# Seven block products instead of eight in the whole experts of a state-space and router kernel

## The chip, the cores and the metric

The kernel runs on one core of a Trainium2 chip. The metric is the device time of one execution in microseconds (us). Three runs of the kernel before took 296.1, 296.74 and 298.02 us; the median is 296.74. A further execution was profiled; all rows below are from it.

In the profile PE is TensorE (PEld its weight loads), DVE is VectorE, ACT is ScalarE, POOL is GpSimd, SP is SyncE, which issues most loads.

## The reference: what is computed

A Mamba-2 state-space block (4 batches, 8 heads, 768 steps) produces 3072 tokens of 256 values. A cosine router sends each token to one of 8 experts, and the expert is a multilayer perceptron (MLP) of two layers, 256 to 1024 to 256:

```python
logits = xn @ en.T / tau
expert_idx = np.argmax(logits, axis=1)
...
gate_w = probs[np.arange(N), expert_idx]
for e in range(E):
    mask = expert_idx == e
    h = np.maximum(x[mask] @ w1[e], 0.0)
    out[mask] = gate_w[mask, None] * (h @ w2[e])
```

All of it is in 32-bit floating point.

## The kernel before, in words

The first 97 us compute the state-space block and the routing, and scatter the tokens into a table in DRAM, sorted by expert. This stage isn't changed. The change lies in the stage behind it, `moe` (L789).

Each expert has 416 places: 4 tiles of 104 tokens. The work is cut into ten parts. Parts 0 to 3 are half experts (experts 0 and 1, two tiles or 208 tokens each; the first half starts before all tokens are routed). Parts 4 to 9 are the six whole experts 2 to 7, 416 tokens each. Tokens that don't fit would go through `leftover` (L899), a loop whose number of turns is read from a table that `leftover_blocks` (L841) computes on VectorE. With this data the loop makes no turn, but its branch is executed.

A part (`part`, L803) runs in an order written out by hand; inside `manual_schedule` every engine executes its instructions in the order of the code:

- **First layer**, `up` (L734): for each of 8 blocks of 128 hidden values, two matmuls (the 256 inputs are two halves of 128) into a PSUM tile `hp`. ReLU moves the result to SBUF as `hT`, on ScalarE (L744) for even blocks and on VectorE (L746) for odd ones.
- Between the blocks, `out` (L768) turns the results of the part before back to rows, scales them by the gate on VectorE (L776) and ScalarE (L778), and writes them to DRAM with an indirect DMA issued by GpSimd (L780).
- `measure` (L682 on) prepares the gate: squares on ScalarE (L692) and a `pow` on GpSimd (L696).
- `turn_x` (L716) transposes the tokens of the next part on TensorE and copies them to SBUF on VectorE (L727).
- `prepare` (L700 on) finishes the gate: some ten small VectorE instructions, with an Exp on ScalarE (L710) among them.
- **Second layer**, `down` (L748): for each half of the 256 outputs, 8 matmuls into a PSUM tile `yp`, copied to SBUF by ScalarE (L762) and VectorE (L764).

Weights are loaded by SyncE three parts ahead (`load_weights`, L203). GpSimd does nothing in this stage but the `pow`, the indirect writes and a tiny memset before each write. In the last part the second layer is split by tokens, so that the rows of its first half are written while the second half is computed.

Of the kernel before, what the change touches and what calls it, by code (L numbers as in the profile page):

```python
# [8 lines left out]
F32 = mybir.dt.float32  # L9
I32 = mybir.dt.int32  # L10
BF16 = mybir.dt.bfloat16
ACT = mybir.ActivationFunctionType
ALU = mybir.AluOpType
# [10 lines left out]
KD, KF = DM // 128, F // 128  # L24
TR, NT = 104, 4
# [3 lines left out]
EE, EC, HT = 2, 4, 2  # L29
LEFT = (T - CAP) // Q + E  # L30

LG, Y1, TOK, W = 128, 128 + E, DM + E, DM + 2 * E
# [106 lines left out]
def between(k):  # L139


    nc = k.nc
    n = NC - 1
    ps = k.pz[:, 1, 448:512]
    for b in range(NB):
        nc.tensor.matmul(  # L146
            ps[:, 16 * b : 16 * b + 16], lhsT=k.spread[:, b, :], rhs=k.parts[:].rearrange("p v k g -> p (v k g)"),
            start=True, stop=True,
        )
    sides = k.mc.tile([128, NB, 2, 8], F32, name="sides")  # L150
    nc.vector.tensor_copy(out=sides[:].rearrange("p b v c -> p (b v c)"), in_=ps)
    k.whole = k.mc.tile([128, NB, n], F32, name="whole")
    nc.vector.tensor_tensor(out=k.whole[:], in0=sides[:, :, 0, 0:n], in1=sides[:, :, 1, 1:NC], op=ALU.mult)
    k.blocks = k.mc.tile([128, NB * n, 2 * 4], F32, name="blocks")
    nc.vector.tensor_tensor(
        out=k.blocks[:], in0=k.whole[:].rearrange("p b k -> p (b k)").unsqueeze(2).to_broadcast([128, NB * n, 8]),
        in1=k.own[:].rearrange("p v q -> p (v q)").unsqueeze(1).to_broadcast([128, NB * n, 8]), op=ALU.mult,
    )
# [44 lines left out]
def load_weights(k, e):  # L203
    k.w1t[e] = k.wp.tile([128, KD, F], F32, name="w1", tag="w1")
    k.nc.sync.dma_start(k.w1t[e][:], k.w1[e].rearrange("(k p) f -> p k f", p=128))
    k.w2t[e] = k.wp.tile([128, KF, DM], F32, name="w2", tag="w2")
    k.nc.sync.dma_start(k.w2t[e][:], k.w2[e].rearrange("(f p) m -> p f m", p=128))
# [449 lines left out]
class Job:  # L657
# [58 lines left out]
    def turn_x(s, ps=None):  # L716
        k, nc, tr, nt = s.k, s.k.nc, s.tr, s.nt
        s.xT = (s.pool or k.p).tile([128, KD, nt * tr], F32, name="xT", tag="xT")
        n = nt * tr
        for j in range(KD):  # L720
            t = s.turned()[:, 0:n] if ps is None else ps[:, n * j : n * j + n]
            for i in range(nt):
                nc.tensor.transpose(
                    t[:, tr * i : tr * i + tr], s.x[:, i, Y1 * j : Y1 * j + 128], k.ident[:tr, :tr]
                )
            if ps is None:
                nc.vector.tensor_copy(out=s.xT[:, j, :], in_=t)  # L727
        if ps is not None:
            nc.scalar.copy(out=s.xT[:].rearrange("p j n -> p (j n)"), in_=ps[:, 0 : KD * n])

    def turned(s):
        return s.k.ps.tile([128, 512], F32, name="turned", tag="turned", bufs=3)

    def up(s, f, ps=None):  # L734
        k, nc, n = s.k, s.k.nc, s.nt * s.tr
        if f == 0:
            s.hT = (s.pool or k.p).tile([128, KF, n], F32, name="hT", tag="hT")
        t = k.ps.tile([128, n], F32, name="hp", tag="hp", bufs=3)[:] if ps is None else ps[:, 0:n]
        for j in range(KD):
            nc.tensor.matmul(  # L740
                t, lhsT=s.w1[:, j, 128 * f : 128 * f + 128], rhs=s.xT[:, j, :], start=(j == 0), stop=(j == KD - 1)
            )
        if f % 2 == 0 or ps is not None:
            nc.scalar.activation(s.hT[:, f, :], t, ACT.Relu)  # L744
        else:
            nc.vector.tensor_scalar_max(s.hT[:, f, :], t, 0.0)  # L746

    def down(s, first, n, between=None):  # L748

        k, nc = s.k, s.k.nc  # L750
        if first == 0:
            s.yT = k.p.tile([128, KD, s.nt * s.tr], F32, name="yoT", tag="yoT")
        c = slice(s.tr * first, s.tr * (first + n))
        for j in range(KD):
            t = k.ps.tile([128, n * s.tr], F32, name="yp", tag="yp", bufs=2)
            for f in range(KF):
                nc.tensor.matmul(  # L757
                    t[:], lhsT=s.w2[:, f, 128 * j : 128 * j + 128], rhs=s.hT[:, f, c],
                    start=(f == 0), stop=(f == KF - 1),
                )  # L760
            if j % 2 == 0:
                nc.scalar.copy(out=s.yT[:, j, c], in_=t[:])  # L762
            else:
                nc.vector.tensor_copy(out=s.yT[:, j, c], in_=t[:])  # L764
            if j == 0 and between:
                between()

# [18 lines left out]
            k.tc.add_to_no_dep_group("out", d.ins)  # L786


def moe(k):  # L789
    parts = [(j, k.early_has[:TR, e, :]) for e, j in enumerate(k.early)]  # L790
    for e in range(EE):
        parts.append((Job(k, HT, TR, k.w1t[e], k.w2t[e]), k.late_has[:TR, e, :]))
    n = E + EE

    def begin(i):
        e = i - EE
        if e < EE:
            parts[i][0].load(k.p.tile([TR, HT, W], F32, name="xg", tag="xg"), T * e + HT * TR)
        else:
            parts.append((Job(k, NT, TR, k.w1t[e], k.w2t[e]), k.has[:TR, e - EE, :]))  # L800
            parts[i][0].load(k.p.tile([TR, NT, W], F32, name="xg", tag="xg"), T * e)

    def part(i):  # L803
        j, has = parts[i]
        last = parts[i - 1][0]
        for f in range(KF):
            j.up(f)
            if 1 <= f and 2 * (f - 1) < last.nt:
                last.out(2 * (f - 1), 2)
            if f == 3:  # L810
                j.measure()
        if i + 1 < n:
            parts[i + 1][0].turn_x()
        j.prepare(has)
        if i + 1 < n:
            j.down(0, j.nt)
        if i == EE + 2:
            leftover_blocks(k)
        if 0 <= i - EE < E - 3:
            load_weights(k, i - EE + 3)  # L820
        if i + 3 < n:
            begin(i + 3)

    with k.tc.manual_schedule():
        begin(EE)
        begin(EE + 1)
        parts[1][0].turn_x()
        parts[0][0].down(0, HT)
        for i in range(1, n - 2):
            part(i)  # L830
    leftover(k)
    with k.tc.manual_schedule():
        for i in range(n - 2, n):
            part(i)
        j = parts[n - 1][0]
        j.down(0, NT // 2)
        j.down(NT // 2, NT // 2, between=lambda: j.out(0, NT // 2))
        j.out(NT // 2, NT // 2)


def leftover_blocks(k):  # L841
# [57 lines left out]
def leftover(k):  # L899
    nc = k.nc  # L900
    table, rf, nf = k.left
    SP = mybir.EngineType.SP
    blocks = nc.values_load(table[0:1, 1, 0:1], min_val=0, max_val=LEFT)
    with k.tc.If(blocks > 0):  # L904
        with k.tc.For_i(0, blocks, 1) as i:
            e = nc.values_load(table[0:1, 0, bass.ds(i, 1)], engines=(SP,), min_val=0, max_val=E - 1)
            w1 = k.wp.tile([128, KD, F], F32, name="w1", tag="w1")
            nc.sync.dma_start(w1[:], k.w1[bass.ds(e, 1)].rearrange("o (k p) f -> p (o k) f", p=128))
            w2 = k.wp.tile([128, KF, DM], F32, name="w2", tag="w2")
            nc.sync.dma_start(w2[:], k.w2[bass.ds(e, 1)].rearrange("o (f p) m -> p (o f) m", p=128))  # L910
            j = Job(k, 1, Q, w1, w2)
            has = k.p.tile([128, 1], I32, name="left_has", tag="left_has")
            nc.vector.tensor_tensor(out=has[:], in0=k.part[:], in1=nf[:, bass.ds(i, 1)], op=ALU.is_lt)
            r = k.p.tile([128, 1], F32, name="left_p", tag="left_p")
            nc.vector.tensor_tensor(out=r[:], in0=k.part[:], in1=rf[:, bass.ds(i, 1)], op=ALU.add)
            at_f = k.p.tile([128, 1], F32, name="left_atf", tag="left_atf")
            nc.vector.memset(at_f[:], float(E * T))
            nc.vector.copy_predicated(at_f[:], has[:], r[:])
            at = k.p.tile([128, 1], I32, name="left_at", tag="left_at")
            nc.vector.tensor_copy(out=at[:], in_=at_f[:])  # L920
            x = k.p.tile([128, 1, W], F32, name="left_x", tag="left_x")
            nc.vector.memset(x[:], 1.0)
            j.gather(x, at)
            j.turn_x()
            j.measure()
            j.prepare(has[:])
            for f in range(KF):
                j.up(f)
            j.down(0, 1)
            j.out(0, 1)  # L930
# [88 lines left out]
```

## Time and profile before

| What | us |
|---|---|
| median of three runs | 296.74 |
| time of the profiled execution | 297.09 |
| its span, first to last instruction | 294.7 |
| state-space block and routing, up to the first second layer (97.44) | 97.4 |
| one whole expert, first layer with transposes (187.94 to 200.71) | 12.77 |
| one whole expert, second layer (200.71 to 211.90) | 11.19 |
| last matmul of a second layer ends | 285.35 |
| last indirect write issued until | 289.26 |

The span is what the profiler saw on the core; the time of the same execution is 2.4 us longer. The mean clock that TensorE was granted is 0.983 of full speed. A line such as `97.44 5.81 PE L757 MATMUL yp<-hT,w 128*128 128x208 f32 x32` gives start, duration from first start to last end, engine, source line, operation, output and inputs, tile, moving shape and number of records. A matmul in 32-bit floating point leaves two records, so x32 are 16 matmuls. Ends of matmuls are modelled and reach a little into the next one.

### The profile page before, as it was taken

Reading aid. Unit: us, or ns where it says so; the run is one execution under the profiler, and the core shown is the slowest. Engines: PE = TensorE matmul, PEld = TensorE weight load, DVE = VectorE, ACT = ScalarE, POOL = GpSimd, SP = SyncE. Lnnn points to the kernel's source line nnn. Section 1 sums busy time; section 2 is a strip of 40 time slices with the busy share of each in tenths; the row PEclk is TensorE's granted clock in tenths of the full one; section 3 lists DMA queues with packets and bytes.
Section 4 is the critical chain, followed back from the end, with each engine's and each line's share of the span. In section 5 each row is a group of like instructions: output and inputs, shape, how many; then the busy total and the mean of one; then the engine's idle time right before and its main releaser. Section 6 shows DMA issues by size and latency. Waiting matters only on the chain.

```text
span 294.7 us, 4832 instructions
## 1 busy us (share of the span) xinstructions
PE 266.5 (90%) x1828; PEld 192.8 (65%) x1828; DVE 125.8 (43%) x403; ACT 77.2 (26%) x211; POOL 93.0 (32%) x172
## 2 busy tenths in 40 slices
PE   0887999999887999999999999999999989999980
PEld 0665887887765899999555555555555545555970
DVE  7576897998622143423240743133034023212310
ACT  2312444533333131331410320040051023014110
POOL 8005436955345230330300070070051015007032
PEclk9999899999999999999999999999999999999995
DMA  6988398931131310385705416334352001001011
GB/s 170 364 308 295 106 362 287 398 130 53 64 101 57 118 31 0 80 281 176 234 11 196 142 47 208 90 113 104 108 174 57 20 3 49 0 0 56 2 29 29
DMA packets 18226, 37.24 MB, mean 126 GB/s; under 512 B 2042, under 2 KB 10439, under 8 KB 18202
## 3 DMA queue, kind: packets, MB, share of 16 engines
q1 hardware_dynamic: 15338, 30.36, 31.1%
q0 software_dynamic: 2688, 6.50, 6.8%
q8 instruction: 15, 0.25, 0.3%
q10 hardware_dynamic: 176, 0.06, 0.1%
q14 instruction: 9, 0.07, 0.1%
HBM read 26.80 MB, written 10.37 MB: 126 GB/s over the span
## 4 chain that ended last, share of the span: by engine, by line
issue 46%; PE 17%; POOL 14%; DMA 11%; DVE 9%; ACT 1%; POOLq 0%; ACTq 0%; DVEq 0%
DMA out_dram<-yo,to 11%; POOL out_dram L780 8%; PE pg L315 4%; DVE g L321 3%; PE pz L369 3%; PE py L351 3%; POOL rows L595 3%; POOL gr L696 2%; PE pf L250 2%; PE py L337 2%; DVE bp L224 1%; PE pf L268 1%; PE pz L234 1%; DMA a<-in_a_dram 1%; PE pz L146 1%
## 5 line engine op out<-in xcount | busy, mean ns | idle before, releaser
L757 PE MATMUL yp<-hT,w 128*128 128x208 f32 (+1 forms) x352 | 91.6, 418 | 0.0
L740 PE MATMUL hp<-xT,w 128*128 128x416 f32 (+1 forms) x288 | 88.0, 455 | 1.9 <-DVEq L904 1.4
L757 PEld LDWEIGHTS yp<-hT,w 128*128 128x128 f32 x352 | 63.5, 190 | 24.2 <-issue 24.2
L780 POOL DMA_INDIRECT out_dram<-yo,to x32 | 32.6, 1017 | 145.9 <-DVE yo L776 141.2
L740 PEld LDWEIGHTS hp<-xT,w 128*128 128x128 f32 x288 | 52.2, 190 | 29.3 <-issue 27.3
L746 DVE TENSOR_SCALAR hT<-hp 128x416 f32<-128x416 f32 (+1 forms) x36 | 18.7, 519 | 55.5 <-PE hp L740 50.3
L744 ACT ACTIVATE hT<-hp 128x416 f32<-128x416 f32 (+1 forms) x36 | 16.5, 459 | 76.6 <-PE hp L740 72.2
L764 DVE COPY yoT<-yp 128x208 f32<-128x208 f32 (+1 forms) x11 | 5.2, 473 | 63.1 <-PE yp L757 63.1
L595 POOL DMA_INDIRECT rows<-yt,row_of x24 | 23.8, 990 | 25.0 <-issue 12.1
L321 DVE TENSOR_TENSOR g<-pg,mask 128x1024 f32<-128x1024 f32 x24 | 28.2, 1218 | 5.6 <-PE pg L315 5.5
L315 PE MATMUL pg<-cm,bt 32*128 32x256 f32 x192 | 20.6, 450 | 0.0
L260 ACT ACTIVATE cm<-cp,tmask 128x256 f32<-128x256 f32 x24 | 10.9, 500 | 21.0 <-DVE cp L255 19.8
L369 PE MATMUL pz<-turn,yT 128*128 128x136 f32 x96 | 15.2, 304 | 1.0 <-ACT yT L361 1.0
L369 PEld LDWEIGHTS pz<-turn,yT 128*128 128x128 f32 x96 | 12.8, 201 | 4.9 <-issue 2.7
L315 PEld LDWEIGHTS pg<-cm,bt 32*128 32x128 f32 x192 | 14.4, 210 | 0.9 <-issue 0.7
L351 PE MATMUL py<-g,x 128*32 128x128 f32 x384 | 13.5, 277 | 0.2 <-issue 0.2
L762 ACT COPY yoT<-yp 128x208 f32<-128x208 f32 (+1 forms) x11 | 4.5, 411 | 30.6 <-PE yp L757 30.6
L297 POOL TENSOR_TENSOR T<-V,blocks 128x256 f32<-128x256 f32 x20 | 11.8, 618 | 0.0
L250 PE MATMUL pf<-f,spread 32*128 32x128 f32 x48 | 10.5, 349 | 1.2 <-DVE V L282 0.6
L692 ACT ACTIVATE sq<-xg 104x256 f32<-104x256 f32 x28 | 11.2, 406 | 0.0
L351 PEld LDWEIGHTS py<-g,x 128*32 128x32 f32 x384 | 10.4, 112 | 1.1 <-issue 0.5
L778 ACT ACTIVATE yo<-turned,gate 104x256 f32<-104x256 f32 x16 | 7.6, 473 | 13.6 <-PE turned L773 13.5
(174 smaller groups left out, 244.2 us busy)
## 6 DMA issues: line engine op xcount, KB each, us to landing
w<-in_moe_w_dram SPq DMA_DIRECT2D x16, 1024.0 KB
rows<-none SPq DMA_DIRECT2D x8, 442.0 KB
x<-in_x_dram SPq DMA_DIRECT2D x6, 512.0 KB
xg<-rows SPq DMA_DIRECT2D x6, 442.0 KB
b<-in_B_dram SPq DMA_DIRECT2D x6, 256.0 KB
ct<-in_CT_dram SPq DMA_DIRECT2D x6, 256.0 KB
out_dram<-yo,to POOLq DMA_INDIRECT x32
xe<-rows SPq DMA_DIRECT2D x2, 221.0 KB
```

The source lines that it names most:

```text
L250: nc.tensor.matmul(k.pf[:, 256 + 128 * i : 384 + 128 * i], lhsT=k.spread[g : g + 32, b + i, :], rhs=k.f[g : g + 32, c // 4, :], start=True ...
L297: k.nc.gpsimd.tensor_tensor(out=T[:], in0=k.V[c][:, b, :].rearrange("p (t d) -> p t d", t=2).unsqueeze(2).to_broadcast([128, 2, 4, D]), in ...
L315: nc.tensor.matmul(k.pg[:, q, 256 * i : 256 * i + 256], lhsT=s.bt[r, i, :], rhs=s.cm[r, i], start=True, stop=True, tile_position=(32 * q, 0),)
L321: nc.vector.tensor_tensor(out=g[:], in0=k.pg[:, :, 256 * i : 256 * i + 256].rearrange("p q (t i) -> p q t i", t=2), in1=k.mask[:].unsqueez ...
L351: k.nc.tensor.matmul(k.py[32 * q : 32 * q + 32, 2 * i + v, :], lhsT=t.x[:, b + i, n : n + 32], rhs=s.g[i][:, q, v, :], start=(c == 0 and i ...
L369: k.nc.tensor.matmul(k.pz[:, i, at : at + Y1], lhsT=yT[:, 2 * i + j, :], rhs=k.turn[:, j, :], start=(j == 0), stop=(j == 1), skip_group_ch ...
L595: d = nc.gpsimd.indirect_dma_start(out=k.rows[:, :], out_offset=bass.IndirectOffsetOnAxis(ap=k.to[g][:, u : u + 1], axis=0), in_=k.yt[:, N ...
L740: nc.tensor.matmul(t, lhsT=s.w1[:, j, 128 * f : 128 * f + 128], rhs=s.xT[:, j, :], start=(j == 0), stop=(j == KD - 1))
L744: nc.scalar.activation(s.hT[:, f, :], t, ACT.Relu)
L746: nc.vector.tensor_scalar_max(s.hT[:, f, :], t, 0.0)
L757: nc.tensor.matmul(t[:], lhsT=s.w2[:, f, 128 * j : 128 * j + 128], rhs=s.hT[:, f, c], start=(f == 0), stop=(f == KF - 1),)
L780: d = nc.gpsimd.indirect_dma_start(out=k.out[:, :], out_offset=bass.IndirectOffsetOnAxis(ap=s.to[:, i : i + 1], axis=0), in_=y[:], in_offs ...
```

## The change

The six whole experts (parts 4 to 9) get a job class of their own, `Seven`. Each of the two matrix products of the expert is seen as a product of 2 by 2 blocks, and is computed with seven block products and extra sums instead of eight block products (the Winograd form of Strassen's method):

- The **weights** are cut in four blocks a[0] to a[3]; four combinations m[0] to m[3] are computed on GpSimd (`mix`), for both layers, each instruction on 128 partitions x 512 values. The combinations for a part are ordered on GpSimd's queue at the start of the part before it.
- The **tokens** are cut in two by the input half and in two by token; four differences `dx` are computed on VectorE (`mix_x`) behind the copies of `turn_x`.
- `up` now works on four groups `g`. In each, seven matmuls of 208 columns go to four PSUM tiles; three of them add to a tile that has been read already (`first=False`). Five sums per group are done on VectorE, one copy and three ReLUs on ScalarE. One of the four result blocks gets its ReLU only where it is used.
- Between the layers, four differences `dh` of the hidden values are computed on VectorE (`mix_h`, 128 x 832 values each).
- `down` has seven products of four matmuls each, with two copies on ScalarE and five sums on VectorE. `measure` stands behind the second product, and the copies of the next part's tokens, its `mix_x` and `prepare` (all of `rest`) behind the fourth.

Around it: the PSUM tiles `hp` (3) and `yp` (2) become one ring `sum` of five; `hT` has one buffer; the copies of `turn_x` become a method `turn_copies`; `leftover_blocks` moves from the end of part 4 to the end of part 1; `leftover` is inside the manual schedule; the last part writes its four tiles of rows together at the end instead of two and two.

```diff
+class Seven(Job):
+    def mix(s, name, a):
+        m = s.k.p.tile([128, 4, KF // 2, 128], F32, name=name, tag=name)
+        for out, in0, in1, op in (
+            (m[:, 0], a[2], a[3], ALU.add), (m[:, 1], m[:, 0], a[0], ALU.subtract),
+            (m[:, 2], a[2], a[0], ALU.subtract), (m[:, 3], a[1], m[:, 1], ALU.subtract),
+        ):
+            s.k.nc.gpsimd.tensor_tensor(out=out, in0=in0, in1=in1, op=op)
+        return m
...
+    def mix_x(s):
...
+        for i, in0, in1 in ((0, b[1], b[0]), (1, b[1], b[3]), (2, b[3], d[:, 0]), (3, b[2], d[:, 2])):
+            nc.vector.tensor_tensor(out=d[:, i], in0=in0, in1=in1, op=ALU.subtract)
...
+    def add(s, in0, in1, out=None):
...
+        s.k.nc.vector.tensor_tensor(out=out, in0=in0, in1=in1, op=ALU.add)
+    def keep(s, ps):
...
+        s.k.nc.scalar.copy(out=out, in_=ps)
...
+    def up(s, g):
...
+        x, y, z, w = (s.sum()[:, 0:h] for _ in range(4))
+        s.product([g], x, a, 0, b, 0)
+        x1 = s.keep(x)
+        s.product([g], y, m, 1, d, 2)
+        q = s.add(y, x1)
+        s.product([g], z, m, 0, d, 0)
+        u = s.add(z, q)
+        s.product([g], w, m, 2, d, 1)
+        s.add(w, u, o[:, 3])
+        nc.scalar.activation(o[:, 3], o[:, 3], ACT.Relu)
+        s.product([g], x, a, 1, b, 2, False)
+        nc.scalar.activation(o[:, 0], x, ACT.Relu)
+        s.product([g], z, m, 3, b, 3, False)
+        s.add(z, q, o[:, 1])
+        s.product([g], w, a, 3, d, 3, False)
+        s.add(w, q, o[:, 2])
+        nc.scalar.activation(o[:, 2], o[:, 2], ACT.Relu)
+
+    def mix_h(s):
...
+        for i, j in ((0, 0), (1, 3)):
+            nc.vector.scalar_tensor_tensor(
+                out=d[:, i], in0=h[:, 1], scalar=0.0, in1=h[:, j], op0=ALU.max, op1=ALU.subtract
+            )
+        nc.vector.tensor_tensor(out=d[:, 2], in0=h[:, 3], in1=d[:, 0], op=ALU.subtract)
+        nc.vector.tensor_tensor(out=d[:, 3], in0=h[:, 2], in1=d[:, 2], op=ALU.subtract)
+
+    def down(s, measured, rest):
...
+        x, z, w, y = (s.sum()[:, 0:n] for _ in range(4))
+        s.product(gs, x, a, 0, b, 0)
+        x1 = s.keep(x)
+        s.product(gs, z, m, 0, d, 0)
+        z1 = s.keep(z)
+        measured()
+        s.product(gs, w, m, 2, d, 1)
+        t = s.add(w, z1)
+        s.product(gs, y, m, 1, d, 2)
+        q = s.add(y, x1)
+        s.add(t, q, o[3])
+        rest()
+        s.product(gs, x, a, 1, b, 2, False)
+        nc.scalar.copy(out=o[0], in_=x)
+        s.product(gs, w, a, 3, d, 3, False)
+        s.add(w, q, o[2])
+        s.product(gs, z, m, 3, b, 3, False)
+        s.add(z, q, o[1])
...
     def part(i):
...
+        if i == EE:
+            parts[2 * EE][0].mix_up()
+        elif new_seven:
+            if i >= 2 * EE:
+                new.mix_up()
+            new.mix_down()
...
-        if i == EE + 2:
+        if i == 1:
             leftover_blocks(k)
...
-        j = parts[n - 1][0]
-        j.down(0, NT // 2)
-        j.down(NT // 2, NT // 2, between=lambda: j.out(0, NT // 2))
-        j.out(NT // 2, NT // 2)
+        parts[n - 1][0].out(0, NT)
```

## The prediction

> **What bounds the kernel now.** I read the page's busy times first, then the table of stages, then TensorE's timeline. Columns of the stages: window, length, busy time (instructions) of PE, PEld, DVE, ACT, POOL, clock, DMA share, GB/s.
>
> ```profile
> PE 266.5 (90%) x1828; PEld 192.8 (65%) x1828; DVE 125.8 (43%) x403; ACT 77.2 (26%) x211; POOL 93.0 (32%) x172
> ...
> 187.94:200.71 12.77, 12.77 (x50) 7.51 (x48) 4.04 (x10) 4.53 (x14) 5.40 (x9) 1.00 0.38 115
> 200.71:211.90 11.19, 11.19 (x34) 6.10 (x33) 2.39 (x12) 0.74 (x2) 0.00 (x0) 1.00 0.43 134
> ...
> 97.44 5.81 PE L757 MATMUL yp<-hT,w 128*128 128x208 f32 x32
> 103.09 1.57 PE L740 MATMUL hp<-xT,w 128*128 128x208 f32 x8
> ...
> 151.99 11.36 PE L757 MATMUL yp<-hT,w 128*128 128x416 f32 x32
> 163.19 2.96 PE L740 MATMUL hp<-xT,w 128*128 128x416 f32 x8
> ```
>
> One whole expert takes 12.77 (first layer, transposes) + 11.19 (second) = 23.96 us. TensorE is busy through both at full clock; VectorE works 6.4 us of it, GpSimd 5.4. TensorE sets the pace, so a block product saved counts in full only if VectorE, ScalarE and GpSimd can follow.
>
> **Part 1, fewer multiplications.** 16 matmuls of 208 columns take 103.09-97.44 = 5.65 us, 0.353 each; 16 of 416 take 11.20, 0.700 each. (Each matmul leaves two records.) An expert goes from 32 x 0.700 = 22.40 to 56 x 0.353 = 19.77: 2.63 saved, 15.8 in six experts. TensorE alone would need 21.3 per expert.
>
> **Part 2, the circle inside a first layer.** Each group of seven products (7 x 0.353 = 2.47) now contains a chain. Prices: ScalarE copy or ReLU of 208, 0.33 (L762, 0.333) or 0.34; VectorE sum of 208, 0.38 (between 0.39 for 128x224, L850, and 0.37 for L746); the next dependent VectorE instruction 0.03 later (L850: 165.44, 0.38 long, next at 165.86); a wait across engines about 0.05 (ReLU ends 92.76, matmul starts 92.81); a result is read 0.20 after its matmul's slot (103.09 to 103.29). ScalarE takes its queue in order: the copy of the next group's x stands behind this group's last ReLU. So: keep x 0.33+0.05, q 0.38, u 0.41, o3 0.41+0.05, product w' 0.35+0.20, sum 0.38+0.05, ReLU 0.34, next keep: 2.95 us, against 2.47 of matmuls. In the two groups with output rows, a 0.47 scaling (L778) enters the circle: 3.4, against 2.47+0.43. Four groups: 2 x 3.4 + 2 x 2.95 = 12.7. With 0.7 of transposes and 28 x 0.353 = 9.9 an expert takes 23.3 if nothing waits at its end: only 0.7 of the 2.63 is left. The h differences, four of 128x832 at about 1.02 (by 0.39 for 224 and 1.21 for 1024 elements), hide under the transposes and the first products.
>
> **Part 3, VectorE's list in the second layer.** Times from that layer's start, D. The fourth product is read at D+5.85. Behind it in VectorE's order stand q and o3 (to 6.6), two copies (1.08 by L727: 7.7), four x differences (1.4: 9.1), preparation to the Exp (about 1.0: 10.1), Exp and its return (0.5), the gate (0.6: 11.2), and only then the last two sums, to 11.9. TensorE ends the layer at 9.9. The next layer's y needs the tile that ScalarE copies behind that Exp (10.9, due 10.3), z the tile of VectorE's last sum (11.9): some 1.4 lost, half of it slack of the circle's first group. 23.3 + 0.8 = 24.1: **an expert would cost what it does now**.
>
> **Part 4, GpSimd's sums stop VectorE.** Eight sums of 128x512 per expert come on GpSimd, where the next instruction behind the old `pow` is the next expert's first sum. The row that decides is in the first stage, where VectorE's L224 (two SBUF inputs, normally 0.275 to 0.284) met four GpSimd sums (L297):
>
> ```profile
> 54.10 2.38 POOL L297 TENSOR_TENSOR T<-V,blocks 128x256 f32<-128x256 f32 x4
> ...
> 54.03 1.97 DVE L224 TENSOR_TENSOR bp<-b,rT 128x128 f32<-128x128 f32 x1
> ...
> 54.03 2.59 DVE L224 TENSOR_TENSOR bp<-b,rT 128x128 f32<-128x128 f32 x2
> ...
> L321 DVE TENSOR_TENSOR g<-pg,mask x24: 1208/1215/1225, 16.9 to 77.8; 128x1024 f32<-128x1024 f32 x24
> ```
>
> Two that need about 0.5 together took 2.59. The first ran only near 55.8, after three of the four sums; the second ended at 56.62, after the fourth. The same shows at 64.77 (2.05 for the pair). L321, with one input in PSUM, keeps 1.21 to 1.23 throughout. So a VectorE instruction with two SBUF inputs waits for the sums already on their way. In the change these are o3, the x differences, the predicated copy and the small product of the preparation, and the h differences; sums from PSUM aren't.
>
> One GpSimd sum of 512: 0.61 for 256 elements (L297, every 0.57) bounds it by 1.22 above and, with 0.1 fixed as in a memset (0.09), by 1.04 below; I take 1.15, eight are 9.2. Every second one waits for the one before it, so they go as 1, 2, 2, 2, 1 with a gap where VectorE gets in. When: the second result is copied by D+3.4, four squares (144.91 to 146.5: 1.6) to 5.0, `pow` (1.05) to 6.1. The train begins just when o3 does. o3 waits to 7.25; copies to 8.7; x differences end at about 10.2, 12.8, 15.4 and 16.8; preparation, Exp and gate 2.1, last sums 0.75: 19.6 instead of 11.9. TensorE stands still for **7.5 us more**, at the start of whole experts 1 to 5, where each time the sums for the following one run (the sixth has none behind it). Before the first there is no o3, so some 6 there: 6 + 4 x 7.5 = 36. If GpSimd's instructions never queued and VectorE took turns with single ones, seven waits of at most 1.15 less what PSUM work covers, about 5.5 a time: 27. If the whole train went first, 9.2 + 6.1 + 3.2 + 2.9 = D+21.4: 9.5 a time, 47.
>
> [...]
>
> **Part 5, single items.** The list of leftover blocks (163.90 to 169.70: 5.8 on VectorE) moves from expert 2, where it cost TensorE 0.52 (170.34), into the last half expert, ahead of its second ReLU. That ReLU comes at 121.5 instead of 116.8; five sum tiles turn, the seventh product needs this tile at 119.8: 2.1, net +1.6 (0 to 3). The leftover branch: TensorE idles 1.38 now (237.40), and started 0.75 after VectorE's last copy; afterwards it starts as late behind VectorE's last sum: 0 to +1, I take 0.5. The weight loads and row loads that follow later preparation on SyncE have a whole expert's time ahead: 0. The merged PSUM pool frees no wait now visible: 0.
>
> The end: four rows now go out together.
>
> ```profile
> 286.17 0.48 DVE L776 TENSOR_SCALAR yo<-turned,gate 104x256 f32<-104x256 f32 x1 [0.41 <-PE turned L773]
> ...
> 286.95 1.00 POOL L780 DMA_INDIRECT out_dram<-yo,to  x1 [1.36 <-DVE yo L776]
> 287.94 0.09 POOL L779 MEMSET tick<- 1x1 f32 x1
> 288.26 1.00 POOL L780 DMA_INDIRECT out_dram<-yo,to  x1 [0.23 <-issue]
> ```
>
> Before, two follow the last product, 1.31 apart; four cost 2 x 1.31 = +2.6.
>
> **Sum.** 297.1 (profiled execution: span 294.7 and 2.4 around it; 0.35 over the median 296.74) + 6 x 0.15 (24.1 for 23.96) + 1.6 + 0.5 + 2.6 = 302.7 without part 4, and with its 36, 338.5. Against the median and for waits that overlap the branch I say **337**. Its own range: 27 to 47 in part 4 gives 329 to 349.
>
> **Rivals.** *The wait stays short:* the train and the x differences miss each other (GpSimd starts early or late) or GpSimd yields at once: 302, still slower, by the circle, the list and the tail. For it: the rows show the wait for 128x128 and 128x256 only. *Faster:* the multiplications alone bound it, because the circle runs faster than the rows add up to and no list waits: 297.1 - 15.8 + 1.6 + 0.5 + 2.6 = 286. It decides once a group's circle is under 2.47 and the train ends before D+6; against it stand 2.95 and `pow`'s place behind the squares. *Not what its title says:* GpSimd sums weights for the first layers only. The diff and the order of instructions show eight per expert, both layers; were it four, the wait would halve: 320. *The whole train goes first:* 349.
>
> **Chances.** The forecast (329 to 346) 0.66, the whole train or worse 0.09, half the wait 0.05, 302 (298 to 312) 0.14, faster 0.06. Range: 302 to 346. A measurement tells 1% from no change, 3 us: faster by over 1% 0.05, within 0.05, slower 0.90.
>
> **What would show it.** Right: x differences on VectorE, 0.38 alone, lasting 2 to 3 us beside GpSimd sums; TensorE idle 6 to 10 us after the first product of experts; groups 2.9 to 3.4 apart; GpSimd sums about 1.15; last four rows 1.31 apart. Wrong: x differences at 0.38 beside running sums, sums far from 1.15, groups 2.5 apart, or a train that starts long before D+6.

## The result, and the profile after

The changed kernel takes 337.51 us (median of four runs, 335.92 to 340.44) beside 296.42 for the kernel before on the same chip (295.47 to 298.02): a ratio of 1.139, 95% interval 1.128 to 1.150. It is slower, and 0.5 us from the forecast of 337. The experiments show that this closeness is partly luck: one term was too large, and one that the prediction doesn't have made up for it. Medians and ratios leave out the few runs that took over 1.5% more than the fastest of the same kernel.

The profiled execution took 340.44 us, with a span of 338.7, which is 44.0 more than before. The mean granted clock of TensorE is 0.929 (0.983 before). From the page, the busy times and the new sums on GpSimd:

```profile
PE 275.4 (81%) x2084; PEld 243.4 (72%) x2084; DVE 233.0 (69%) x570; ACT 95.6 (28%) x294; POOL 154.4 (46%) x220
...
L806 POOL TENSOR_TENSOR m<-w 128x512 f32<-128x512 f32 x24 | 31.6, 1317 | 1.4 <-DMA out_dram<-yo,to 1.4
```

TensorE's share falls from 90% to 81%. It waits more, and it is also busy for longer, though there is less to multiply. VectorE was busy for 125.8 us and now is for 233.0. A sum of this group takes 1.32 us as a mean.

Where did the 44.0 us go? The starts of the ten second layers, taken from the two TensorE timelines, tell it:

| from one second layer's start to the next | before | after | more |
|---|---|---|---|
| start of the program to the first (97.44, 98.37) | 97.44 | 98.37 | 0.93 |
| half experts 1, 2 and 3 together | 36.58 | 40.40 | 3.82 |
| into whole expert 1 | 17.97 | 24.15 | 6.18 |
| into whole expert 2 | 24.75 | 31.73 | 6.98 |
| into whole expert 3 | 23.97 | 31.44 | 7.47 |
| into whole expert 4 | 23.96 | 32.46 | 8.50 |
| into whole expert 5, with the leftover branch | 25.58 | 35.01 | 9.43 |
| into whole expert 6 | 23.24 | 23.24 | 0.00 |
| last second layer and end | 21.2 | 21.9 | 0.7 |

Five intervals hold 38.6 of it. Each holds the start of a first layer (whole experts 1 to 5) during which GpSimd computes the combinations for the following expert. Into expert 6 no combinations are computed, and nothing is lost. TensorE's timeline of one such start (start, duration, operation, in brackets the idle time before it and what ended it; the second layer begins at D = 194.65):

```profile
203.12 1.57 PE L829 MATMUL sum<-h,m 128*128 128x208 f32 x8
204.52 0.52 PE L829 MATMUL sum<-xT,w 128*128 128x208 f32 x2
206.46 0.59 PE L829 MATMUL sum<-dx,m 128*128 128x208 f32 x2 [1.42 <-DVE dx L825]
211.81 1.80 PE L829 MATMUL sum<-dx,m 128*128 128x208 f32 x4 [4.76 <-ACT yoT L907]
213.41 0.90 PE L829 MATMUL sum<-xT,w 128*128 128x208 f32 x2
```

The first product (204.52) needs only tokens and weights. The second needs a token difference and comes 1.42 late. The third needs a PSUM tile that ScalarE still has to read (L907; ScalarE makes three copies in a second layer, where the section on the change says two) behind its Exp, which stands behind VectorE's list: 4.76 more. The prediction had this wait one product earlier. Then even the products themselves are slow: 0.90 for a product (a pair of records) that takes 0.52 above. VectorE's timeline of the same time:

```profile
200.91 1.32 DVE L837 TENSOR_TENSOR yoT<-part 128x208 f32<-128x208 f32 x1
202.16 1.07 DVE L731 COPY xT<-turned 128x416 f32<-128x416 f32 x2
203.16 1.80 DVE L825 TENSOR_TENSOR dx<-xT 128x208 f32<-128x208 f32 x2
204.89 2.78 DVE L825 TENSOR_TENSOR dx<-xT,dx 128x208 f32<-128x208 f32 x2
...
207.71 1.10 DVE L704 COPY_PREDICATED to_f<-has,xg 104x4 f32<-104x4 int32 x1
208.84 1.19 DVE L706 CAST to<-to_f 104x4 int32<-104x4 f32 x1
...
210.35 0.92 DVE L709 TENSOR_TENSOR gl<-gl,gr 104x32 f32<-104x32 f32 x1
...
212.09 0.62 DVE L837 TENSOR_TENSOR yoT<-sum,part 128x208 f32<-128x208 f32 x2
```

And GpSimd's:

```profile
200.74 1.26 POOL L806 TENSOR_TENSOR m<-w 128x512 f32<-128x512 f32 x1
...
204.69 1.40 POOL L806 TENSOR_TENSOR m<-w,m 128x512 f32<-128x512 f32 x1
...
209.97 1.25 POOL L806 TENSOR_TENSOR m<-w,m 128x512 f32<-128x512 f32 x1
```

The train of eight sums runs from 200.74 to 211.2. Eight VectorE instructions meet it: the last of the first four results, four differences, the predicated copy, the cast, and the small product. Alone they take 0.17 to 0.4; here each lasts until the running GpSimd sum ends and 0.02 to 0.23 longer. That is 0.9 to 1.4 for seven of them; the first difference begins near the end of a sum and takes 0.44. The copies from PSUM (202.16, 0.54 each) aren't held. The list's last sums end at D + 18.06.

The granted clock is the last column but two in the windows of the same core (window, length, busy time and instructions of PE, PEld, DVE, ACT, POOL, clock, DMA share, GB/s):

```profile
204.52:211.81 7.29, 1.11 (x5) 0.49 (x5) 6.79 (x11) 0.50 (x3) 6.66 (x7) 0.77 0.20 59
211.81:215.40 3.59, 3.59 (x10) 3.20 (x11) 2.27 (x8) 0.81 (x3) 0.00 (x0) 0.51 1.00 347
215.40:225.37 9.97, 9.45 (x51) 7.85 (x50) 6.31 (x18) 4.21 (x14) 4.30 (x7) 1.00 0.40 132
```

For 3.59 us after the stall TensorE runs at half its clock (0.51): at most 3.59 x 0.49 = 1.8 us lost, on top of 1.42 + 4.76 = 6.2 of idle time. Together that is up to 8.0; the interval that holds this start is 7.47 longer than before.

### The profile page after: what moved, and what is told of

It is laid out like the page before. It is cut to its first block, busy times and chain, and to the rows that moved or that the text cites. A ratio compares the mean times of both kernels' runs of the same rounds, so it can differ in the third digit from the quotient of the medians.

```text
span 338.7 us, 5793 instructions
## 1 busy us (share of the span) xinstructions
PE 275.4 (81%) x2084; PEld 243.4 (72%) x2084; DVE 233.0 (69%) x570; ACT 95.6 (28%) x294; POOL 154.4 (46%) x220
## 4 chain that ended last, share of the span: by engine, by line
issue 29%; PE 24%; DMA 17%; POOL 17%; DVE 10%; ACT 2%; POOLq 0%; ACTq 0%; DVEq 0%
DMA out_dram<-yo,to 15%; POOL m L806 10%; POOL out_dram L785 5%; PE sum L762 5%; PE pg L315 4%; PE sum L745 3%; DVE g L321 3%; PE pz L369 2%; PE pg L745 2%; PE pf L250 2%; PE py L351 1%; PE py L337 1%; DMA xe<-rows 1%; DVE bp L224 1%; POOL gr L696 1%
## 5 line engine op out<-in xcount | busy, mean ns | idle before, releaser
L829 PE MATMUL sum<-dx,m 128*128 128x208 f32 x144 | 35.2, 380 | 22.0 <-ACT yoT L907 14.3
L829 PEld LDWEIGHTS sum<-dx,m 128*128 128x128 f32 x144 | 28.2, 213 | 25.4 <-ACT yoT L907 15.4
L837 DVE TENSOR_TENSOR part<-sum,part 128x208 f32<-128x208 f32 x60 | 22.4, 374 | 25.7 <-PE sum L829 17.5
L837 DVE TENSOR_TENSOR h<-sum,part 128x208 f32<-128x208 f32 x72 | 27.0, 375 | 15.5 <-PE sum L829 11.5
L595 POOL DMA_INDIRECT rows<-yt,row_of x24 | 23.8, 990 | 25.8 <-issue 13.4
L829 PE MATMUL sum<-xT,w 128*128 128x208 f32 x96 | 27.6, 373 | 9.0 <-DVEq L1051 9.0
L806 POOL TENSOR_TENSOR m<-w 128x512 f32<-128x512 f32 x24 | 31.6, 1317 | 1.4 <-DMA out_dram<-yo,to 1.4
L829 PE MATMUL sum<-dh,m 128*128 128x208 f32 x144 | 26.4, 340 | 0.1
L829 PEld LDWEIGHTS sum<-xT,w 128*128 128x128 f32 x96 | 18.8, 214 | 9.5 <-issue 9.3
L829 PEld LDWEIGHTS sum<-dh,m 128*128 128x128 f32 x144 | 25.3, 190 | 0.4 <-issue 0.4
L762 PE MATMUL sum<-hT,w 128*128 128x208 f32 x128 | 23.5, 342 | 0.0
L762 PEld LDWEIGHTS sum<-hT,w 128*128 128x128 f32 x128 | 22.6, 193 | 0.0
L315 PE MATMUL pg<-cm,bt 32*128 32x256 f32 x192 | 21.3, 461 | 0.0
L745 PE MATMUL sum<-xT,w 128*128 128x208 f32 x96 | 19.3, 355 | 1.9 <-DVE hT L751 1.9
L745 PEld LDWEIGHTS sum<-xT,w 128*128 128x128 f32 x96 | 17.6, 198 | 2.2 <-DVE hT L751 2.2
```

The costliest lines, as they stand in the source:

```text
L315: nc.tensor.matmul(k.pg[:, q, 256 * i : 256 * i + 256], lhsT=s.bt[r, i, :], rhs=s.cm[r, i], start=True, stop=True, tile_position=(32 * q, 0),)
L595: d = nc.gpsimd.indirect_dma_start(out=k.rows[:, :], out_offset=bass.IndirectOffsetOnAxis(ap=k.to[g][:, u : u + 1], axis=0), in_=k.yt[:, N ...
L745: nc.tensor.matmul(t, lhsT=s.w1[:, j, 128 * f : 128 * f + 128], rhs=s.xT[:, j, :], start=(j == 0), stop=(j == KD - 1))
L762: nc.tensor.matmul(t, lhsT=s.w2[:, f, 128 * j : 128 * j + 128], rhs=s.hT[:, f, c], start=(f == 0), stop=(f == KF - 1),)
L806: s.k.nc.gpsimd.tensor_tensor(out=out, in0=in0, in1=in1, op=op)
L829: s.k.nc.tensor.matmul(ps, lhsT=lhsT(i, g), rhs=rhs(j, g), start=(first and g == gs[0]), stop=(g == gs[-1]), skip_group_check=True,)
```

## The experiments

My theory (A): the combinations on GpSimd, computed while VectorE has its list to do, stop VectorE and through it TensorE, at five starts. Rivals: the loss is in the order of the seven products itself, in the circle inside a first layer, or in VectorE's longer list even without GpSimd.

**Without the repeated sums.** The combinations are computed for the first whole expert only, and every later one uses those again.

```diff
-        m = s.k.p.tile([128, 4, KF // 2, 128], F32, name=name, tag=name)
+        if name in s.k.mixed:
+            return s.k.mixed[name]
+        m = s.k.mixed[name] = s.k.p.tile([128, 4, KF // 2, 128], F32, name=name, tag=name)
```

> Left out: GpSimd computes the weight combinations for the first whole expert only, and the other five use the same ones (so what they compute is not the reference). Everything else is as in the changed kernel. Theory A (GpSimd's sums hold up every VectorE instruction with two SBUF inputs): the x differences fall to 0.38 us each, TensorE's idle time at the starts of whole experts 2 to 4 falls from 6.2 us to about 1.4, at the start of the fifth from 9.0 to about 2.8, and its clock stays up there: about 305 us in all (300 to 311). Rival B (VectorE's list in the second layer is simply too long, GpSimd beside it doesn't matter): the idle times stay, 330 to 338 us.

Measured: 301.1 us, ratio 1.009 (1.005 to 1.012). The repeated sums cost 36.4 us by the medians (38.7 by the two ratios, each taken against the kernel before on its own chip), and everything else in the change together 2.5 to 3.7. Per expert it takes 23.7 to 23.9. In this kernel's VectorE timeline the differences are short:

```profile
212.95 0.65 DVE L827 TENSOR_TENSOR dx<-xT 128x208 f32<-128x208 f32 x2
213.52 0.78 DVE L827 TENSOR_TENSOR dx<-xT,dx 128x208 f32<-128x208 f32 x2
```

**The same sums, later.** Here all sums are computed, but a tiny copy on GpSimd, placed ahead of a train, reads the last result of the expert before. So the train can't start until VectorE's list is done.

```diff
             if i >= 2 * EE:
+                y = last.yT[0:1, 0, 4 * TR - 1 : 4 * TR] if isinstance(last, Seven) else last.yT[0:1, KD - 1, 0:1]
+                k.nc.gpsimd.tensor_copy(out=k.tick[:], in_=y)
                 new.mix_up()
```

> Nothing is left out. GpSimd's eight sums for the next expert begin only when the last result of the expert before has been written (a one-element copy of that result stands in front of them), so they run beside the first layer, whose VectorE sums read PSUM, instead of beside the end of the second layer. Theory A: as with the sums left out, about 305 us, and up to 2 us per expert more if the end of the sums meets the h differences: 300 to 315. Rival B: 333 to 340. A third view, C (what counts is how much GpSimd does in all, not when): also 333 to 340.

Measured: 299.52 us, ratio 1.006 (1.002 to 1.009). All the work of the change is there, and all but 2 of its 41 us are gone. It isn't the amount of GpSimd work that costs time, but when it runs. GpSimd and VectorE in this kernel:

```profile
216.38 1.26 POOL L806 TENSOR_TENSOR m<-w 128x512 f32<-128x512 f32 x1
```

```profile
212.39 0.65 DVE L825 TENSOR_TENSOR dx<-xT 128x208 f32<-128x208 f32 x2
```

The train now lies beside a first layer, where VectorE's sums read PSUM and keep their 0.38. Theory A holds, and the rivals fall as the main cause.

**One layer at a time.** In one kernel the first layer has eight products again and the second layer seven; in the other it is the reverse. Each has four sums a train. The core of the two edits, the second layer alone first:

```diff
-        for f in range(KF // 2 if seven else KF):
+        for f in range(KF):
             j.up(f)
...
-            if new_seven:
-                new.mix_x()
```

```diff
-    def down(s, measured, rest):
+    def down(s, first, n):
...
+            for f in range(KF):
+                nc.tensor.matmul(
+                    t.rearrange("p (t n) -> p t n", t=2), lhsT=s.w2[:, f, 128 * j : 128 * j + 128],
+                    rhs=s.h[:, 2 * (f % 2) : 2 * (f % 2) + 2, f // 2, :],
+                    start=(f == 0), stop=(f == KF - 1),
+                )
```

> The first layer is undone: eight products of 416 columns as before, with no token differences and no first-layer sums on GpSimd; the second layer keeps its seven products and four GpSimd sums per expert. By theory A: the four sums (5.3 us) still hold up o3, the predicated copy, the cast and the small product, the list ends at D+13.5 instead of D+18, TensorE waits about 2.2 us per start instead of 6.2 and isn't idle long enough to lose its clock: 22.65 + 2.2 per expert, with the moved leftover list (+3.8) and the tail (+2.2) about 307 us (302 to 311). By rival B (the list alone, 1.4 us shorter without the x differences): 325 to 332, since TensorE would wait 5 us per start.

> The second layer is undone: eight products of 416 columns, no h differences, no second-layer sums; the first layer keeps its seven products and four GpSimd sums. VectorE's list then has 9 us of slack under the second layer, held up or not. What is left is the circle of the first layer: groups 2.9 to 3.4 us apart, 12.7 + 0.7 + 11.2 = 24.6 per expert against 23.96, with the moved leftover list (+3.8) and the tail (+2.2) about 307 us (303 to 311). If the circle doesn't bound it (groups 2.5 apart, 2.9 with output rows), 23.1 per expert: about 298.

Measured: 293.99 us with the second layer alone, ratio 0.986 (0.979 to 0.992), a little faster than before and 13 below what I expected; 306.27 with the first layer alone, ratio 1.027 (1.021 to 1.033), as expected. For the first of them, GpSimd's timeline shows the miss:

```profile
189.71 1.26 POOL L806 TENSOR_TENSOR m<-w 128x512 f32<-128x512 f32 x1 [4.02 <-PE sum L829]
```

The train waits for TensorE, which still reads the second layer's combinations from the buffer that the train is to fill. So it starts with the next first layer (189.46) and meets no list. The buffer does here what the tiny copy did above. TensorE then needs 22.64 us per expert instead of 23.96: the multiplications are worth what they should be where nothing stands in their way. With the first layer alone an expert takes 24.7 (transposes at 206.33 and 231.04), because of the circle inside that layer. Whether or not its four sums hold VectorE, TensorE doesn't wait there (the next first layer begins at 218.24 with no idle time before it): that second layer needs nothing from VectorE's list.

**The leftover list and the end.** On the kernel with seven products in the second layer only, `leftover_blocks` goes back to its old place, and in a further kernel the last rows are also written two and two.

```diff
-        if i == 1:
+        if i == EE + 2:
             leftover_blocks(k)
```

```diff
-        s.product(gs, z, m, 3, b, 3, False)
+        if rows:
+            s.product(gs[:2], z, m, 3, b, 3, False)
+            s.out(0, s.nt // 2)
+            s.product(gs[2:], z, m, 3, b, 3, False)
...
-        parts[n - 1][0].out(0, NT)
+        parts[n - 1][0].out(NT // 2, NT // 2)
```

> The kernel with seven products in the second layer only, with the list of leftover blocks put back to where it was before the change (behind whole expert 1). Leaves nothing out. If the move cost what the changed kernel's trace shows, 15.90 us for the last half expert instead of 12.08 (1.9 us of idle time and the rest matmuls at half clock behind it), and the list costs 0.5 us at its old place: 3.3 us less than the 294.0 of the same kernel with the list moved, 290.7 (289 to 292.5). If only the idle time counted, as the prediction had it (1.6): 292.4.

> The same with the end of the last expert split again: its first two row tiles are turned and written in the middle of the last product, the other two after it. Leaves nothing out. By the prediction's price for the merged end (2 x 1.31 = 2.6 us, 2.2 in the trace): 288.3 (287 to 290). If the end is set by something else than the four writes in a row: 290.7.

Measured: 292.06 (ratio 0.981, 0.974 to 0.989) and 291.26 (0.978, 0.971 to 0.985). The list's move cost 1.9 us by the medians. By the spans it is 2.9 (293.1 to 290.2), but 1.0 of that lies ahead of the first second layer (98.57 and 97.57), before the list. 292.06 is nearer to the 292.4 of the idle time alone than to the 290.7 with the half clock, because the list isn't free at its old place either: TensorE waits 1.44 us for it there (172.86). So this pair doesn't show what the half clock costs. In the changed kernel the half experts take 3.82 longer; 1.88 of it is idle time of TensorE, and behind it the clock is at half (for 3.41 us from 123.15). The split end brought 0.6 by the spans, not 2.2 to 2.6: four writes 1.31 apart still follow the first one, and that comes only 0.6 earlier.

**Seven products in both layers, in another order.** Both layers have seven products; the sums wait as in the second experiment; the list is in its old place and the end is split; and the circle is cut: the first product of the next group (`first`) is issued ahead of the last two of this one, and two of the ReLUs move behind the layer.

```diff
-        x, y, z, w = (s.sum()[:, 0:h] for _ in range(4))
-        s.product([g], x, a, 0, b, 0)
-        x1 = s.keep(x)
+        x, x1 = s.next
+        y, z, w = (s.sum()[:, 0:h] for _ in range(3))
...
-        nc.scalar.activation(o[:, 3], o[:, 3], ACT.Relu)
         s.product([g], x, a, 1, b, 2, False)
         nc.scalar.activation(o[:, 0], x, ACT.Relu)
+        if g + 1 < KF // 2:
+            s.first(g + 1)
```

> Nothing is left out. Seven products in both layers, GpSimd's sums behind the last result of the expert before, list and end as before the change, and the first layer's circle cut: the next group's first product and its copy stand ahead of this group's last two products (the fifth PSUM tile holds it), and the ReLUs of two of the four blocks are done for all groups at once behind the layer. The longest chain from group to group is then w' 0.35, y 0.55, q 0.41, u 0.41, o3 0.43 = 2.15 us, under the 2.47 of the seven products. If the circle of the prediction is what held the first layer at 3.1 to 3.45 us per group: groups at 2.5 and 2.9, some 22.0 us per expert instead of 23.7, 285 to 288 us in all. If the rate of VectorE (19.4 us of work per expert) or another wait holds it: groups stay over 2.9, 290 to 294.

Measured: 301.33 us, ratio 1.011 (1.003 to 1.018). Experts 3 and 4 take 22.06 and 22.01 us and groups 2.47 and 2.90, as expected. But one wait of 13.08 us appears in expert 2. TensorE, VectorE and GpSimd:

```profile
177.48 1.03 PE L829 MATMUL sum<-xT,m 128*128 128x208 f32 x2 [13.08 <-DVE part L837]
```

```profile
167.43 1.41 DVE L1013 TENSOR_TENSOR mine<-begin,step 128x224 f32<-128x224 f32 x1
168.76 1.44 DVE L1013 TENSOR_TENSOR mine_not<-end,step 128x224 f32<-128x224 f32 x1
```

```profile
167.34 1.26 POOL L806 TENSOR_TENSOR m<-w,m 128x512 f32<-128x512 f32 x1
```

The leftover list, where the instructions shown take 0.39 each when they run alone, now meets the train that was moved. The list lasts from 163.16 to 176.58, 13.4 us where it took 5.8 before. So some 7.6 come from the train, by the same mechanism at a new place, and the rest is the list itself, which stands ahead of the sums that TensorE needs. Whoever moves the train has to look at what else stands in VectorE's queue there.

**The list in pieces.** The list becomes a generator and is issued in eight pieces between the first-layer blocks of the last two half experts.

```diff
+        if i == 2:
+            k.steps = leftover_blocks(k)
         for f in range(KF // 2 if seven else KF):
             j.up(f)
+            if i in (2, 3) and f % 2 == 1:
+                next(k.steps, None)
...
-        if i == EE + 2:
-            leftover_blocks(k)
```

> Edit on the kernel of e8_reordered: the leftover list leaves the place between two whole experts, where it met the gated sums, and is issued in eight pieces of three to five instructions between the first-layer results of the last two half experts. Theory (the 13.08 us wait of e8_reordered was the list beside GpSimd's train, with the half clock behind it): 13.1 of wait and some 1.8 of half clock go from its span of 300.2, 285.3 is left, 287 us as a time (286 to 289), 0.965 of the kernel before; every whole expert takes 22.0 to 22.1. Rival (the wait is VectorE's own order in the first layers, which the list only happened to meet): the wait stays in the second whole expert or comes back in another, 298 to 301 us. Second rival: the pieces hold up the half experts by what they take, 5 to 6 us, 291 to 293.

Measured: 285.76 us (284.77 to 287.48), ratio 0.961 (0.958 to 0.964). This version beats both kernels: 11.4 us less than before. From its page, and two windows that reach from one second layer's start to the next (columns as above):

```profile
PE 255.3 (89%) x2084; PEld 231.7 (81%) x2084; DVE 198.9 (70%) x570; ACT 93.6 (33%) x258; POOL 159.4 (56%) x225
```

```profile
175.59:197.64 22.05, 21.96 (x130) 20.81 (x129) 17.48 (x49) 8.16 (x25) 16.77 (x19) 1.00 0.41 134
197.64:219.66 22.02, 21.98 (x131) 20.83 (x129) 17.51 (x49) 8.17 (x25) 16.79 (x19) 1.00 0.41 135
```

A whole expert takes 22.0 us, with TensorE busy throughout and at full clock, GpSimd's work the same as in the changed kernel, and VectorE busy for 17.5.

**Filling the stall.** On the changed kernel, 12 matmuls into an unused tile follow the first product of whole experts 2 to 4, so that TensorE is idle for only 2.2 us there.

```diff
+        if g == 0 and s.fill:
+            t = s.turned()[:, 0:h]
+            for i in range(12):
+                nc.tensor.matmul(t, lhsT=s.a1[0][:, 0], rhs=s.bx[0], start=True, stop=True)
```

> The changed kernel with twelve matmuls (4.2 us) that write a PSUM tile nobody reads, behind the first product of whole experts 2 to 4, where TensorE otherwise stands idle for 6.2 us. They add work and leave nothing out. If the half-speed matmuls after these stalls come from the idle time itself (granted clock 0.51 from 211.81 to 215.40), the clock stays at full speed there and each of the three starts is 1.8 us shorter: about 332 us (330 to 334.5). If the clock drops for another reason, or the loss is hidden by VectorE's list anyway: 337 or, with the added work, more.

Measured: 337.88 us, ratio 1.133 (1.124 to 1.141): no gain that can be told. The windows behind the second and the third of the filled stalls:

```profile
211.68:215.35 3.67, 3.52 (x10) 3.03 (x11) 2.28 (x8) 0.81 (x3) 0.00 (x0) 0.57 0.97 328
...
243.26:246.35 3.09, 2.84 (x14) 2.09 (x15) 2.51 (x9) 0.79 (x3) 0.00 (x0) 1.00 0.99 337
```

Of the three starts one kept the full clock. The three intervals that hold them take 31.86, 31.59 and 30.52. The one at full clock is 1.1 to 1.3 shorter than the other two, and 1.9 shorter than the same interval in the changed kernel (32.46), where TensorE ran at half clock for 6.2 us; the other two are as long as there (31.73, 31.44). So the half clock costs some 1 to 2 us a start, less than half of its length, and my fill wasn't a sure way round it.

**How long does one VectorE instruction wait?** The prediction took "through the sums already on their way" from the row at 54.03; the timeline above shows turns with single sums. Two kernels cut each sum of 512 values into two of 256 or four of 128 (steps of 1 in the second), the same values in all.

```diff
-            s.k.nc.gpsimd.tensor_tensor(out=out, in0=in0, in1=in1, op=op)
+            for f in range(0, KF // 2, 2):
+                g = slice(f, f + 2)
+                s.k.nc.gpsimd.tensor_tensor(out=out[:, g], in0=in0[:, g], in1=in1[:, g], op=op)
```

> Edit on the kernel after: each GpSimd sum of 128x512 is cut in two of 128x256, sixteen a train in place of eight, the same values. VectorE's eight held instructions per second layer (o3, four x differences, predicated copy, cast, gl) now end its list 6.8 us late (D+18.05 for some D+11.3). Turns with single sums: each waits for at most one sum of about 0.65, the delay is about halved, 3.4; TensorE stands 2.8 per start where it stands 6.2: 4.5 starts x 3.4 = 15 less, 322 us (315 if the clock then stays full, 327 if the train grows by its fixed costs). Queue of sums, as the row at 54.03 of the kernel before reads (there a VectorE instruction waited through three sums of 0.57): with halves a sum no longer waits for the one just ahead of it, the train isn't interrupted, a held instruction waits 1.9 or more: 337 to 349 us.

> Edit on the kernel after: each GpSimd sum of 128x512 is cut in four of 128x128, thirty-two a train. Turns with single sums: at most about 0.35 of wait for each of eight VectorE instructions, a delay of some 1.5 to 2, last sums at D+13: TensorE stands under 1.5 per start, 308 to 316 us; the train itself grows to 11 or 12 us and reaches further into the next first layer, where sums from PSUM aren't held. Queue of sums: as with halves, 337 to 349 us.

Measured: 344.67 (ratio 1.161, 1.159 to 1.164) and 347.60 (1.171, 1.168 to 1.174). Shorter sums made it slower. VectorE with halves, and then with quarters:

```profile
209.22 9.44 DVE L827 TENSOR_TENSOR dx<-xT 128x208 f32<-128x208 f32 x1
```

```profile
204.46 13.26 DVE L839 TENSOR_TENSOR yoT<-part 128x208 f32<-128x208 f32 x1
```

With quarters one VectorE sum, 0.38 us when it runs alone, stood for 13.26, over the whole train of 32 GpSimd sums (204.29 to 217.5). With halves VectorE got in once, after the first sum, and then one difference waited for all the rest. So the row at 54.03, where sums had 256 values, read truly, and what it showed doesn't carry over to 512.

Is it the size, or that with 512 a sum reads the result of the one just ahead of it? In the changed kernel only the second of each four does (`m[:, 1]` reads `m[:, 0]`; `m[:, 3]` reads `m[:, 1]`, two ahead), and yet VectorE got in behind every sum. A last kernel keeps 512 and interleaves the two layers' combinations, so that no sum reads the one ahead of it.

```diff
+    def mix_run(s):
+        n = len(s.sums) // 4
+        for i in range(4):
+            for out, in0, in1, op in s.sums[i : 4 * n : 4]:
+                s.k.nc.gpsimd.tensor_tensor(out=out, in0=in0, in1=in1, op=op)
```

> Edit on the kernel after: the eight sums of a train go in another order, first those of both matrices' first combination, then of the second and so on; all stay 128x512, and none reads the result of the sum just ahead of it. Cut into halves and quarters (e11, e12) the train let VectorE in once or not at all, and one x difference waited 9.4 us; uncut it let VectorE in after every sum. Theory size: what lets VectorE in is the length of a sum, 512 values against 256; the order does nothing, each held VectorE instruction still waits for one sum, 1.1 to 1.4 us, and the time stays 337 (335 to 341). Theory order: what let VectorE in was that a sum waited for the one just ahead of it, which halves and quarters took away as this order does; then one VectorE instruction waits for the rest of the train, 8 to 9 us, and the time goes to 343 to 348.

Measured: 323.84 us, ratio 1.094 (1.087 to 1.102), which neither theory gave. GpSimd and VectorE:

```profile
199.91 1.28 POOL L812 TENSOR_TENSOR m<-w 128x512 f32<-128x512 f32 x1 [2.76 <-PE sum L835]
201.15 2.49 POOL L812 TENSOR_TENSOR m<-m,w 128x512 f32<-128x512 f32 x2
```

```profile
200.17 1.04 DVE L707 TENSOR_SCALAR gr<-gr 104x4 f32<-104x4 f32 x1
...
201.46 1.00 DVE L709 TENSOR_TENSOR gl<-gl,gr 104x32 f32<-104x32 f32 x1
```

The new order put a sum for the second layer in second place, and this one waits 2.76 us for its buffer, as in the kernel with the second layer alone. In that gap all four differences ran. That is why the time fell. The question has its answer in the other rows: VectorE's instructions at 200.17 and 201.46 each waited for one sum only (they end just behind 201.2 and 202.4), though no sum there reads the one ahead of it. So of these two it is the size that decides, not the order. Why 512 values leave a gap and 256 don't, no run here shows.

## Why the prediction was right, and where only in sum

The mechanism and its place were right, the total of part 4 by luck. (302.7 and 36 make 338.7, where the prediction's sum has 338.5.)

**Part 1, multiplications.** Right within 0.7. With nothing in the way an expert takes 22.0 us; TensorE alone was put at 21.3. The 0.7 lies in the first layer (185.46 to 196.93 in the kernel with the list in pieces, 11.47 us, where 28 products of 0.353 and the turning of four row tiles make 10.75).

**Part 2, the circle.** Right in size and mechanism. The groups stand 3.45 apart with output rows and 3.08 without, for 3.4 and 2.95. First layer alone: 24.7 per expert. With the circle cut, 2.90 and 2.47, which is the multiplications alone.

**Part 3, VectorE's list.** The list was right within 0.6: without the repeated sums the last sums end at D + 11.3 (216.67 - 205.40), for 11.9. What it costs was too high: TensorE waits at most 0.24 at a time in the experts there, the branch aside, not 0.8, so that an expert takes 23.7 to 23.9, not 24.1.

**Part 4, GpSimd's sums.** The step that named the mechanism and its place held; its total of 36 met the 36.4 to 38.7 that the repeated sums cost. But two parts of it failed and cancelled:

- The rule "waits for the sums already on their way", with 7.5 a time, was wrong for sums of 512. VectorE took turns with single sums, the case that the prediction set aside at about 5.5 a time and 27 in all. Measured are 6.2 at each of three starts, 3.28 at the first (for 6) and 9.00 - 1.50 = 7.5 at the branch, together 29.3. The list ended at D + 18.06, not D + 19.6. The gaps in the train weren't where the prediction put them ("1, 2, 2, 2, 1"): VectorE got in behind every sum. The train was longer than estimated, 1.27 a sum alone and up to 1.40 in turns for the estimate of 1.15, and it held two kinds that the prediction left free: the cast and, at the fifth start, a 104x4 scaling (272.88, 1.24).
- The half clock behind each stall isn't in the prediction at all. 38.6 of the five intervals less 29.3 of idle time leave 9.3. By windows of 0.1 us TensorE ran at half clock for 3.4, 4.5, 3.5, 6.2 and 6.0 us behind the five stalls, 23.6 in all, which takes at most 11.8. That the actual loss is smaller would fit waits of the circle that fall away while the products are slow; no run separates that.

In the changed kernel each wait ends with one sum of 1.25 to 1.40, so the 27 that the prediction gives for turns with single sums was the better figure for the idle time (29.3). Those are sums of 512. With sums of 128 it doesn't hold: one wait of 13.26 us outlasted 32 instructions. By what means a sum holds VectorE, no run here shows.

**Part 5, single items.** The moved list cost 3.8 in the changed kernel, some 3.0 net of the 0.8 that it had cost at its old place (24.75 for 23.97), where 1.6 net was predicted: its idle time of 1.88 is as worked out (2.1), and the half clock behind it was missing again. The branch costs 0.1 more than before without the repeated sums (1.50 for 1.38), for 0.5. The end: from the end of the last product (327.13) to the end of the last write's issue 6.10 us, 3.91 before (285.35), so 2.2 for the estimate of 2.6.

Without part 4 the sum was 302.7; the two kernels that take its cause away measured 301.1 and 299.5.

**The rivals.** Short waits (302) would have come true with the train 5 us later, as the second experiment shows: the time of that rival was right, its condition not met. The faster case (286) named its condition well: the reordered kernel whose groups take 2.47 and whose train misses the list runs in 285.76. That its number agrees so well is luck: the 286 contains the moved list and the merged end, which that kernel doesn't have in this form, and experts of 21.3, not 22.0. Half the wait and the whole train first didn't happen; quarters of a sum make the latter, 347.60 for its 349.

## What to carry to other kernels

Work given to GpSimd "for free" has to be placed in time: beside VectorE instructions that read PSUM it cost nothing here (299.52 us with all sums, 301.1 without the repeated ones), beside those that read only SBUF it cost 8 us for 10 us of sums (38.6 over five starts). Before moving a train of GpSimd sums, list what stands in VectorE's queue over its whole length, and gate the train if need be; cutting it into shorter instructions made it worse (344.67 and 347.60 us for 337.51). And price a stall of TensorE with what follows it: here 6 us of idle time cost some 8.

## What the hardware showed that I had not expected

- In the changed kernel the granted clock moved on a grid: up to the last matmul it is at half (0.50) six times, for 3.41, 3.41, 6.83, 6.83, 10.24 and 10.24 us (one, two or three times 3.41), from 123.15, 150.45, 177.76, 208.48, 239.20 and 273.33; these starts lie 8, 8, 9, 9 and 10 times 3.41 apart. So how long TensorE ran slowly behind a stall depended on where the stall lay: behind three equal stalls of 4.76 it was 4.5, 3.5 and 6.2 us. The clock also fell to half behind a stall of 1.88 us (ahead of 122.79) and, at two of the three filled starts, behind stalls of 2.2 us.
- VectorE was held by GpSimd's sums of 512 in a cast and a scaling with one SBUF input too (1.19 at 208.84 in the changed kernel and 1.04 at 200.17 in the interleaved one, for 0.17 and 0.16 alone), not only with two.
- GpSimd sums of 256 or 128 values in a row let VectorE in once or not at all (9.44 and 13.26 us of waiting); in the changed kernel sums of 512 let it in after each, and its instructions took 0.9 to 1.4.
- It went the other way too: most of the indirect writes that GpSimd issues while VectorE computes the differences `dh` last 1.5 to 1.9 us instead of 1.01 in the kernels with the later sums (205.71, 1.73 in the first of them).
